# 228 tiny products of nothing at the head of TensorE's program, in place of most of the wide ones

## The chip, the cores and the metric

The kernel runs on one core of a Trainium2 chip. The metric is the device time of one execution in microseconds. TensorE (PE, with its weight loads PEld), VectorE (DVE), ScalarE (ACT), GpSimd (POOL) and SyncE (SP) each run their own program; semaphores and DMA queues tie them together.

## The reference

Three layers follow each other. All is float32.

```python
# attention over 32 memory slots: q, k, v (4, 8, 576, 64), phi (4, 8, 576, 32)
a = np.exp(phi - np.max(phi, axis=2, keepdims=True))
a = a / (np.sum(a, axis=2, keepdims=True) + 1e-09)
k_m = np.einsum('bhsm,bhsd->bhmd', a, k)
v_m = np.einsum('bhsm,bhsd->bhmd', a, v)
scores = np.matmul(q, k_m.transpose(0, 1, 3, 2)) / np.sqrt(64)
attn = softmax(scores)
x = np.matmul(attn, v_m)                    # then (2304, 512)
# gated layer: w_gate, w_val (512, 1536), w_out (1536, 512)
xn = x / np.sqrt(np.mean(x * x, axis=-1, keepdims=True) + 1e-06) * rms_g
x = (silu(xn @ w_gate) * (xn @ w_val)) @ w_out
# second layer: w_in (512, 2048), w_out (2048, 512)
h = x @ w_in
g = np.where(h >= 1, h, np.where(h <= -1, 0.0, (h + 1) ** 2 / 4))
out = g @ w_out
```

## The kernel before, in words

The kernel is one program. Its first part, up to about 440 us, is ordered by a planner that is written out in the kernel (`Agenda`): streams of work (`soft`, `memory`, `pair`, `chunk`, `vw`, `gv`, `out1` and others) yield steps with an engine and a planned duration. The planner takes the step that can start first, by priority among equals, and instructions are issued in that order. The result is a fixed order for every engine; the planned times are not used on the chip.

For each batch b of four, `soft` (line 420) computes the exponentials of phi: DVE takes a maximum (`pm`), PE transposes it (`mps`, line 433), DVE reduces (`gm`) and spreads it (`dg`), PE multiplies by `spread` (line 450), DVE subtracts (line 456), ACT takes the exponential (line 463), and POOL forms the sums `s1`. `memory` (line 492) multiplies the exponentials by k and v: nine steps of eight small float32 products (`kvps`, line 504; 144 PE products in the profile, each with its weight load, because a float32 product is two of them). Its tiles have 64 rows and 32 columns, so four land next to each other in one bank. Two more products (line 517) form the sums of the exponentials. `pair` (line 589) then does the attention of 128 query rows: transposes of q (`qps`, line 612), scores (`sc`, line 630), a softmax on DVE and ACT, transposes (`aTp`, line 672), the product with v's memory (`xp`, line 693), the mean square, and transposes into `Ah` and `Al` (line 717). Inputs arrive by SP's queue in the order phi, k, v of batch 0, q, phi, k, v of batch 1, and so on; there are two buffers each for phi, k with v, and q. Behind the inputs the weights follow in pieces (`raw`), which DVE, ACT and POOL convert in `chunk`.

`heat` (line 477) fills gaps in PE's order with products of a tile of zeros (`zeros`, set by DVE at the start), 128 x 128 weights by 256 columns, which nobody reads. It has the lowest priority. The planner counts PE's planned work in periods of 3.413 us (`TICK`); a wide product of zeros is added in a period only while that period has under 2.09 us of work (`HEAT`), and a period that follows one with over 1.38 us (`WARM`) is planned at full speed, any other at half speed. The stream ends when batch 2's exponentials are planned. Once the attention and the gates are done, PE goes through `out1`, and then a second stage of `hp` and `acc` products that has no planner.

## Time and profile before

| | us |
|---|---|
| median of three runs | 845.07 |
| lowest and highest | 843.63, 845.24 |
| the profiled execution | 843.29 |
| its span, first to last instruction | 841.5 |

Busy time as a share of the span: PE 97%, its weight loads 85%, DVE 53%, ACT 40%, POOL 10%. The span counts from the first to the last instruction; 1.8 us of the profiled execution lie around it. PE and PEld are counted as one instruction each, semaphore instructions are not counted. "issue" in a chain, or as a releaser, is time in which an engine waited for nothing that the profile shows. The DMA table lists traffic by queue; the kind "instruction" is the engines' own program.

### The profile page before, as it was taken

The numbers are of one execution on the slowest core, as the hardware profiler recorded it, in microseconds if no ns is written. First come the engines' busy times: TensorE is split into PE (matmuls) and PEld (weight loads), VectorE is DVE, ScalarE is ACT, GpSimd is POOL, SyncE is SP. The second block draws the span as 40 slices with busy tenths as digits, with TensorE's granted clock in tenths as the row PEclk, the third lists the DMA queues.
The fourth block names the chain that finished last, engine by engine and source line by source line (L and its number), as shares of the span: only waits on it lengthen the run. The fifth ranks groups of instructions, "written<-read, shape, count | busy, mean of one in ns | idle before, by whom it ended". The sixth has DMA issues, their size and how long they took to land.

```text
span 841.5 us, 14910 instructions
## 1 busy us (share of the span) xinstructions
PE 817.0 (97%) x6052; PEld 718.0 (85%) x6052; DVE 449.5 (53%) x788; ACT 337.3 (40%) x635; POOL 82.8 (10%) x133
## 2 busy tenths in 40 slices
PE   7999879999999999999999999999999999999997
PEld 5877767999999999999998888888888888888896
DVE  3678898984776577558214333433343334333443
ACT  1558866763664366435203222222222222222232
POOL 3365400100000000001305100000000000000000
PEclk9999899999999999999999999999999999999999
DMA  9974697885788768786969900100040003000100
GB/s 324 322 245 146 215 309 252 305 280 180 240 281 303 238 225 273 259 268 224 334 221 351 356 0 1 51 1 0 17 134 0 1 1 101 0 1 1 51 1 25
DMA packets 76804, 137.54 MB, mean 163 GB/s; under 512 B 9408, under 2 KB 46272, under 8 KB 76736
## 3 DMA queue, kind: packets, MB, share of 16 engines
q1 hardware_dynamic: 66080, 108.02, 38.7%
q0 software_dynamic: 10496, 28.32, 10.6%
q8 instruction: 47, 0.77, 0.4%
q10 hardware_dynamic: 160, 0.26, 0.1%
q14 instruction: 21, 0.17, 0.1%
HBM read 99.35 MB, written 37.22 MB: 162 GB/s over the span
## 4 chain that ended last, share of the span: by engine, by line
PE 91%; DMA 4%; ACT 2%; DVE 2%; issue 1%; SPq 0%; DVEq 0%; ACTq 0%
PE acc L1129 24%; PE hp L1098 24%; PE ops L920 18%; PE vps L819 8%; PE gps L819 8%; PE vwps L772 3%; PE xp L693 2%; DMA raw<-in_moe_w_val_dram 2%; PE sc L630 2%; DMA kv<-in_v_dram 1%; PE kvps L504 1%; PE qps L612 1%; DMA raw<-in_moe_w_gate_dram 1%; PE heat L484 0%; DVE w L285 0%
## 5 line engine op out<-in xcount | busy, mean ns | idle before, releaser
L1098 PE MATMUL hp<-xh,w 128*128 128x512 f32 (+1 forms) x640 | 193.1, 368 | 0.0
L1129 PE MATMUL acc<-w,gh 128*128 128x512 f32 x576 | 178.4, 391 | 0.0
L1098 PEld LDWEIGHTS hp<-xh,w 128*128 128x128 f32 x640 | 117.0, 188 | 21.5
L1104 DVE SCALAR_TENSOR_TENSOR y<-y 128x512 f32<-128x512 f32 (+1 forms) x80 | 51.1, 639 | 151.4 <-ACT y L1103 151.4
L1129 PEld LDWEIGHTS acc<-w,gh 128*128 128x128 f32 x576 | 107.0, 188 | 22.4
L1098 PE MATMUL hp<-xl,w 128*128 128x512 f32 (+1 forms) x320 | 118.3, 370 | 0.0
L920 PE MATMUL ops<-ah,wo1h 128*128 128x288 f32 x384 | 113.7, 296 | 0.0
L920 PE MATMUL ops<-ah,wo1l 128*128 128x288 f32 x384 | 113.1, 295 | 0.0
L920 PE MATMUL ops<-al,wo1h 128*128 128x288 f32 x384 | 113.1, 294 | 0.0
L1129 PE MATMUL acc<-w,gl 128*128 128x512 f32 x288 | 112.6, 392 | 0.0
L1103 ACT ACTIVATE y<-hp,consts 128x512 f32<-128x512 f32 (+1 forms) x80 | 51.8, 648 | 150.9 <-PE hp L1098 150.9
L1113 ACT ACTIVATE gh<-y 128x512 fp32r<-128x512 f32 (+1 forms) x80 | 47.5, 593 | 137.4 <-PE acc L1129 120.0
L1114 DVE TENSOR_TENSOR gl<-y,gh 128x512 fp32r<-128x512 f32 (+1 forms) x80 | 51.1, 639 | 80.3 <-ACT gh L1113 80.3
L920 PEld LDWEIGHTS ops<-ah,wo1h 128*128 128x128 f32 x384 | 72.0, 188 | 2.5 <-issue 2.5
L920 PEld LDWEIGHTS ops<-al,wo1h 128*128 128x128 f32 x384 | 72.0, 188 | 0.0
L920 PEld LDWEIGHTS ops<-ah,wo1l 128*128 128x128 f32 x384 | 72.0, 188 | 0.0
L1098 PEld LDWEIGHTS hp<-xl,w 128*128 128x128 f32 x320 | 60.3, 188 | 10.8
L1129 PEld LDWEIGHTS acc<-w,gl 128*128 128x128 f32 x288 | 54.0, 188 | 12.3
L819 PE MATMUL vps<-Ah,vwh 128*128 128x288 f32 x192 | 59.4, 309 | 2.4 <-DVE th L875 2.4
L819 PE MATMUL gps<-Ah,vwh 128*128 128x288 f32 x192 | 58.1, 303 | 2.3 <-ACT th L872 2.3
L819 PE MATMUL gps<-Ah,vwl 128*128 128x288 f32 x192 | 57.3, 298 | 0.0
L819 PE MATMUL gps<-Al,vwh 128*128 128x288 f32 x192 | 57.2, 298 | 0.0
(123 smaller groups left out, 1254.1 us busy)
## 6 DMA issues: line engine op xcount, KB each, us to landing
w<-wf_d SPq DMA_DIRECT2D x36, 512.0 KB, 4.9
w<-w_d POOLq DMA_DIRECT2D x36, 512.0 KB, 10.6
w_d<-w2s SPq DMA_DIRECT2D x32, 512.0 KB, 3.8
raw<-in_moe_w_out_dram SPq DMA_DIRECT2D x28, 512.0 KB, 4.8
raw<-in_moe_w_in_dram SPq DMA_DIRECT2D x16, 512.0 KB, 5.1
raw<-in_moe_w_gate_dram SPq DMA_DIRECT2D x12, 512.0 KB, 5.9
raw<-in_moe_w_val_dram SPq DMA_DIRECT2D x12, 512.0 KB, 6.3
wf_d<-w SPq DMA_DIRECT2D x12, 512.0 KB, 3.9
```

Source lines behind the costliest of these rows:

```text
L504: nc.tensor.matmul(out=kvp[g][0][32 * c : 32 * c + 32, 0 : 2 * D], lhsT=ph[gs, c, j, :], rhs=kv[gs, :, c, j, :], start=(j == 0), stop=(j = ...
L630: nc.tensor.matmul(out=scv[rows, z, :], lhsT=qT[:, h, rows], rhs=kmT_t[bb][:, z].rearrange("p j m -> p (j m)"), start=True, stop=True, ski ...
L693: nc.tensor.matmul(out=xp[rows, 256 * g : 256 * g + 256], lhsT=aT[:, i, g, rows], rhs=vbd_t[bb][:, g].rearrange("p h d -> p (h d)"), start ...
L772: nc.tensor.matmul(out=vps[g][0][32 * c : 32 * c + 32, 2 * P * x : 2 * P * x + 2 * P], lhsT=vT[b][hs, c, :], rhs=t[hs, c].rearrange("p i f ...
L819: nc.tensor.matmul(out=p[:, 0:HB], lhsT=wt[:, g, i, :], rhs=at[b][:, g, c], start=(g == 0 and x == 0), stop=(g == 1 and x == 2),)
L920: nc.tensor.matmul(out=p[:, 0:HB], lhsT=wt[:, fc, d], rhs=at[:, c], start=(fc == 0 and x == 0), stop=(fc == NF1 - 1 and x == 2),)
L1098: nc.tensor.matmul(out=hp, lhsT=wt[:, kc, :], rhs=xt[:, kc, 0:n], start=(kc == 0 and x == 0), stop=(kc == KC - 1 and x == 2),)
L1103: nc.scalar.activation(out=y, in_=hp, func=AF.Relu, scale=0.5, bias=half)
L1104: nc.vector.scalar_tensor_tensor(out=y, in0=y, scalar=1.0, in1=y, op0=ALU.min, op1=ALU.mult)
L1113: nc.scalar.activation(out=gh, in_=y, func=AF.Copy)
L1114: nc.vector.tensor_tensor(out=gl, in0=y, in1=gh.bitcast(F32), op=ALU.subtract)
L1129: nc.tensor.matmul(out=acc, lhsT=gt[:, cs], rhs=wt, start=(fc == 0 and x == 0), stop=(fc == NF2 - 1 and x == 2),)
```

## The change

`heat` issues 228 products of 32 x 32 x 64 zeros ahead of its loop, going round the four groups of 32 output partitions of the same bank. Around them it books PE's planned time twice, 3.9 us before they are issued and 2.6 us behind, as a step of kind "Pz" that the planner doesn't lengthen. The loop of wide products follows as it was.

```diff
+BURN = (228, 2.9, 2.6)
...
-                    t *= slow
+                    t *= 1.0 if kind == "Pz" else slow
...
         yield "take", ("bank", HEAT[0])
         t = psum.tile([P, 512], F32, tag=f"b{HEAT[0]}", name="heat")
+        yield "Pz", BURN[1] + 1
+        for n in range(BURN[0]):
+            c = n % 4 * 32
+            nc.tensor.matmul(
+                out=t[c : c + 32, 0:32], lhsT=zeros[0:64, 0:32], rhs=zeros[0:64, 0:32],
+                start=True, stop=True, skip_group_check=True,
+            )
+        yield "Pz", BURN[2]
         while HEAT[1] not in agenda.flags:
             go = yield "heat", 0.1067
```

## Rows read from the trace of the kernel before

**Rows 1.** The page: engines' busy time, the chain's shares, PE's program queue.
```profile
PE 817.0 (97%) x6052; PEld 718.0 (85%) x6052; DVE 449.5 (53%) x788; ACT 337.3 (40%) x635; POOL 82.8 (10%) x133
PE 91%; DMA 4%; ACT 2%; DVE 2%; issue 1%; SPq 0%; DVEq 0%; ACTq 0%
q8 instruction: 47, 0.77, 0.4%
```

**Rows 2.** Stages (length; PE, PEld, DVE, ACT, POOL busy; granted clock; DMA share, GB/s).
```profile
57.00:82.00 25.00, 24.27 (x382) 21.08 (x381) 21.69 (x46) 20.58 (x45) 15.48 (x19) 1.00 0.31 101
140.00:841.00 701.00, 696.26 (x4502) 616.15 (x4494) 347.92 (x591) 252.58 (x464) 33.22 (x54) 1.00 0.44 145
```

**Rows 3.** The chain that ended last in order of time: start, length, what.
```profile
1.77 10.26 DMA kv<-in_v_dram
12.17 2.24 PE kvps L504 x143
15.48 0.33 PE qps L612 x3
15.81 2.86 issue
...
23.66 0.12 PE mps L433
...
27.70 2.25 PE kvps L504 x144
...
41.30 1.47 PE kvps L504 x91
42.77 0.68 issue
...
45.11 1.73 PE xp L693 x8
46.84 0.32 PE kvps L517 x4
...
57.77 2.18 PE kvps L504 x144
```

**Rows 4.** Stages up to the first stop's end, and to the second's.
```profile
0.00:18.60 18.60, 13.01 (x222) 10.03 (x222) 7.43 (x13) 2.44 (x2) 7.03 (x24) 1.00 0.94 316
18.60:43.00 24.40, 23.15 (x381) 20.27 (x382) 14.39 (x32) 11.98 (x23) 9.16 (x12) 0.93 1.09 331
```

**Rows 5.** DMA in windows 16.0:17.2 (two rows), 22.4:23.6, 40.8:42.1, 47.2:48.5, 60.1:61.1 (two rows).
```profile
DMA packets 198, 0.47 MB, mean 390 GB/s; under 512 B 1, under 2 KB 1, under 8 KB 197
q8 instruction: 1, 0.02, 5.7%
...
q8 instruction: 1, 0.02, 5.6%
...
q8 instruction: 1, 0.02, 5.4%
...
q8 instruction: 1, 0.02, 5.5%
...
DMA packets 1, 0.02 MB, mean 16 GB/s; under 512 B 0, under 2 KB 0, under 8 KB 0
q8 instruction: 1, 0.02, 6.5%
```

**Rows 6.** PE in order of time, from the start.
```profile
1.04 6.09 PE L484 MATMUL heat<-zeros 128*128 128x256 bf16 x37 [1.04 <-DVE zeros L355]
```

**Rows 7.** A stage behind the first stop, columns as in rows 2.
```profile
20.00:22.00 2.00, 2.00 (x11) 1.93 (x10) 0.00 (x0) 1.19 (x2) 0.00 (x0) 0.50 1.05 385
```

**Rows 8.** v of batch 1: its issue, its landing after that; DVE's pm of batch 1.
```profile
9.98 2.04 SPq L387 DMA_DIRECT2D kv<-in_v_dram  x1
...
DMA to landing us min/median/max: 13.2/13.2/13.2
...
16.56 2.08 DVE L427 TENSOR_REDUCE pm<-phi 128x128 f32<-128x1152 f32 x1 [0.19 <-DMA phi<-in_phi_dram]
```

## The prediction

> **What bounds the kernel now.** I read the page first. PE is busy for 97% of the span and carries 91% of the chain that ended last; all DMA together has 4% of it [rows 1]. So an edit counts only if it moves PE's own order of work. The table of stages says where that can be: from 140 us to the end PE is busy for 696.26 of 701 us, and nothing there waits. Between 57 and 82 us it is busy for 24.27 of 25 us, and the DMA engines are at a third [rows 2]. In that stretch every engine works through a fixed order and the transfers start when buffers come free, so I see nothing tied to absolute time after about 57 us. A shift of PE's work that stands there should reach the end unchanged. The question is what the change does before 57 us.

> **What is removed and added.** In the planner, 228 tiny products book PE's time up to 6.64 us, over the 2.09 us that HEAT wants in both of the first two planned periods. Of the 37 wide products that open PE's program [rows 6], 36 go, and one is left ahead of the first transpose. From there the plan has the same free times and the same two warm periods, so the order of all later work is the same. PE's program becomes 456 - 72 = 384 instructions longer at its head: 24 KB, which at 390 GB/s is 0.06 us of DMA time. No other queue gets anything.

> **The opening itself.** No row has a 32-column bf16 product of this tile. The nearest are the 144 products of 32 output rows and 128 columns in 2.24 us [rows 3], 15.6 ns each, at full clock. So I bound the 228 between a quarter of 15.6 ns (a quarter of the columns) and twice it (the half clock that rows 7 show elsewhere): 0.9 to 7.1 us, and take 3.6 us, ending near 4.6. About product 222 to 224 ends block 1, and PE waits there. Block 0 ended near product 94, so the packet for block 2 was asked for at about 2 to 2.5 us, when the inputs have just begun; with 3.5 to 6.4 us it is usable at 5.5 to 9. The wide products ended at 7.13 before, and the first transpose came with their end [rows 6]. So this costs 0 to 2 us there, and it is covered: the 144 products that follow wait for v of batch 0 until 12.03 [rows 3], and behind those the chain has 2.86 us that will not be needed. I put this part at 0.

> **Where the block ends fall afterwards.** Counting forward in the old order, less 384:
> - Block 2 ends at about product 92 of the first 144. Its successor was asked for at 5.5 to 9, usable by 9 to 15.4; needed at 12.17 + 92 x 0.0156 = 13.6. Between 0 and 1.8 us late, still covered as above.
> - Block 3 then ends at the second or third of the 144 products that stood at 27.70. The place at 15.81 now has no block end, so the transposes go on and 2.86 us are gained for the moment, with some more since PE's clock need not fall: the granted clock was 0.50 from 20 to 22 us, after that stop [rows 7]. The set can start once v of batch 1 has landed, at 9.98 + 13.2 = 23.2 us [rows 8], and its exponent is done, which before took 27.70 - 23.66 = 4.0 us from the transpose; pm for that is ready at 16.56 + 2.08 = 18.6 [rows 8], near 19.3 behind the products of zeros. So the set starts at about 23.4, 4.3 us early.
> - Block 4 ends at about product 130 of that same set. The sequencer can enter block 4 only when it has passed the wait for v at 23.2, so its successor is asked for at 23.2 and is usable at 23.2 + 6.4 = 29.6. Before, product 130 ran at 27.70 + 130 x 0.0156 = 29.7. The whole gain of 4.3 us is waited away again: -0.1 us.
> - Block 5 ends at about product 27 of the set at 41.30; asked for at 29.6, it is there by 36. The old stop of 0.68 us at 42.77 falls away: -0.7 us, for the moment.
> - Block 6 ends before the last of the eight xp products that end at 46.84 [rows 3]. Its successor is asked for when the sequencer enters block 6, 41.3 to 41.7, and is usable at 47.7 to 48.1. Without the old stop PE would be there near 45.6. So it waits some 2.2 us, and the last xp product ends at 47.7 + 0.25 = 48.0 instead of 46.84: +1.15 us.
> - The next that could be late is asked for near product 45 of the set at 57.77, at 58.5, and by the low end usable at 62.0; it is needed 60 instructions behind that set's end at 59.95, which at that stretch's 763 in 25 us is 61.9 [rows 2, 3]. Nothing is late there, or hardly, and later work needs fewer instructions in a microsecond.

> Sum: 0 - 0.1 - 0.7 + 1.9 = **+1.1 to +1.2 us**, in PE's order at 48 us. What follows (row sums, transposes, the third and fourth memories) starts from that product and from the sums behind it, so I carry it to the end. The profiled execution has a span of 841.5 us and took 843.29, 1.8 us around it; the sum gives a span of 842.65 and 844.4. The median of the three runs is 845.07, 1.8 us above that execution, so in its terms 846.2.

> [...]

> **Rivals.**
> - *The stops go and no new ones come.* If blocks asked for at 23.2 and 41.3 come in 3.5 us, as in idle DMA, the second set ends at 23.2 + 3.5 + 0.2 = 26.9 instead of 29.95, and the later stop is gone too: -3.0 - 0.7 = -3.7 us, 841.4. For it: the first request comes before the inputs fill the queues. Against: over 18.6 to 43.0 the DMA engines are full, share 1.09 [rows 4].
> - *Late blocks cost more.* Each 0.1 us that a block takes beyond 6.4 counts twice, in the second set and again near 46, so the sum passes 1.7 from 6.7 us. With 7.1 us it is +2.5, with 7.7 us +3.7: 847.6 to 848.8. For it: the packet between 40.8 and 42.1 [rows 5] belongs to a block that, counted forward from 18.67, PE entered near 35.8, over 5 us earlier. Against: the packets behind 18.67 and 43.45 came alike, within 0.1 us as far as the windows tell.
> - *Nothing moves by much.* PE passes every block end within 0.5 us because the next block is there, except in places where it would have waited for a buffer or an input anyway (the second set for v at 23.2, the last xp product for its bank near 47): 845.1, from -0.5 to +0.5. For it: 45 of the 47 packets of the kernel before came without a stop that the chain shows; against: 256 instructions pass in 2 us in the sets of 144.

> **How the numbers follow.** A measurement of this kernel can tell about 0.2%, 1.7 us, from no change. Forecast, +0.5 to +1.7: 0.42. Late blocks, over +1.7: 0.25. Little moves: 0.15. Stops gone: 0.18, beyond -1.7. The forecast's upper edge gives 0.02 to slower. So faster 0.18, same 0.40 + 0.15 = 0.55, slower 0.27. The range leaves out the ends of the two outer cases, some 0.1 each: 841.4 to 848.6. The forecast's own is 845.6 to 846.8.

> **What the profile would show.** Right: the stop at 15.81 gone and the granted clock at 1.00 from 18 to 24 us; a stop inside the tiny products near the 223rd; one some 14 products before the second set's end, until 29.6; one before L517 near 46, until 47.7; from 57 us on a constant shift. Wrong: q8's packets within 4 us of a block's start under load, two blocks not being all that is there at first, or a PE order changed beyond the opening.

## The result, and the profile after

The changed kernel takes 850.69 us (median of six, 848.03 to 853.03) against 844.20 for the kernel before (843.63 to 845.24): a ratio of 1.0075, 95% interval 1.0053 to 1.0097. It is 6.5 us slower where +1.1 was forecast and 848.6 was the upper end. The profiled execution took 849.44 us with a span of 847.7, against 843.29 and 841.5. It is one of the quicker of the six: it has a mean granted clock of 0.990, and the four that took 849.88 to 853.03 us have 0.980 to 0.983. What follows is read from the one trace.

The page of the changed kernel, beside [rows 1]: PE's busy time grew by 1.8 us, the chain's share of "issue" from 1 to 2%, and PE's program by two packets.

```profile
PE 818.8 (97%) x6244; PEld 718.7 (85%) x6244; DVE 449.2 (53%) x788; ACT 338.2 (40%) x635; POOL 83.8 (10%) x133
PE 91%; DMA 3%; DVE 2%; ACT 2%; issue 2%; SPq 0%; DVEq 0%; ACTq 0%
q8 instruction: 49, 0.80, 0.4%
```

The chain that ended last in the changed kernel, in order of time (start, length, what); lines of the source are 9 higher than before. It answers to [rows 3].

```profile
1.04 2.02 PE heat L485 x208
3.06 4.90 issue
...
10.63 3.91 PE heat L493 x18
14.54 2.18 PE kvps L513 x144
...
25.63 2.15 PE kvps L513 x130
27.78 2.49 issue
30.27 0.45 PE kvps L513 x14
30.72 2.92 PE sc L639 x16
...
34.15 2.03 PE heat L493 x9
...
44.84 2.18 PE kvps L513 x144
...
49.12 2.26 issue
51.37 0.48 PE xp L702
51.86 0.44 PE kvps L526 x4
52.29 1.90 PE sc L639 x8
...
65.94 2.18 PE kvps L513 x144
...
90.33 1.04 PE vwps L781 x32
...
135.36 5.06 DMA raw<-in_moe_w_gate_dram
...
145.55 0.67 PE vwps L781 x16
```

The stop of 2.86 us among the transposes of q is gone, and so is the one of 0.68 us in the third set of 144 products. In their place PE stops for 4.90 us in the tiny products, 2.49 us behind product 130 of the second set, and 2.26 us ahead of the last xp product. To compare, the same places of the kernel before that were not shown yet:

```profile
29.94 1.93 PE sc L630 x16
...
32.19 1.09 PE heat L484 x9
...
47.15 1.03 PE sc L630 x8
...
82.15 1.04 PE vwps L772 x32
...
128.93 6.91 DMA raw<-in_moe_w_val_dram
...
139.49 0.67 PE vwps L772 x16
```

The 16 sc products took 1.93 us and now take 2.92, nine wide products of zeros 1.09 and now 2.03, the eight sc products 1.03 and now 1.90. None of them waits for anything. The stages of the changed kernel say why (length; PE, PEld, DVE, ACT, POOL busy; granted clock; DMA share, GB/s). The first of them holds the tiny products up to the first stop, 223 products and 224 weight loads:

```profile
0.00:5.00 5.00, 2.02 (x223) 1.92 (x224) 0.40 (x2) 0.18 (x1) 4.11 (x20) 1.00 0.60 188
...
27.70:30.30 2.60, 0.11 (x5) 0.03 (x6) 1.89 (x2) 0.00 (x0) 0.96 (x3) 1.00 1.05 386
30.30:34.00 3.70, 3.70 (x34) 3.38 (x34) 0.00 (x0) 0.00 (x0) 0.00 (x0) 0.65 1.16 289
34.00:37.50 3.50, 3.50 (x19) 2.98 (x19) 2.84 (x12) 0.36 (x1) 1.71 (x2) 0.50 1.11 199
...
45.00:49.10 4.10, 4.10 (x155) 3.39 (x139) 3.08 (x6) 1.91 (x5) 3.87 (x6) 1.00 1.09 372
49.10:51.40 2.30, 0.04 (x2) 0.03 (x1) 0.00 (x0) 0.15 (x2) 0.84 (x1) 1.00 1.07 340
51.40:55.00 3.60, 3.60 (x19) 3.36 (x19) 2.62 (x6) 0.69 (x2) 2.11 (x4) 0.57 1.09 347
55.00:59.00 4.00, 4.00 (x22) 4.00 (x21) 1.27 (x4) 1.79 (x3) 1.02 (x2) 0.53 0.26 85
```

PE was almost idle in each of the two later stops, and behind each the granted clock fell to 0.50 while PE was busy all the time, from 31.4 to 38.3 and from 51.9 to 58.7 us; the rows at 0.65, 0.57 and 0.53 hold part of it. Between the two it was back at 1.00, from 45.0 to 49.1 us. From the starts in the two chains the shift of PE's order can be split (after minus before; the first column names where a stage ends):

| PE's order up to | before | after | shift | added in the stage |
|---|---|---|---|---|
| start of the first set of 144 | 12.17 | 14.54 | +2.37 | +2.37: opening |
| start of the second set | 27.70 | 25.63 | -2.07 | -4.44: old stop gone, and the half clock behind it |
| end of the second set | 29.94 | 30.72 | +0.78 | +2.85: new stop |
| start of the third set | 41.30 | 44.84 | +3.54 | +2.76: half clock |
| sums of the third set | 46.84 | 51.86 | +5.02 | +1.48: stop of 2.26 for one of 0.68 |
| start of the fourth set | 57.77 | 65.94 | +8.17 | +3.15: half clock |
| first vwps | 82.15 | 90.33 | +8.18 | 0 |
| vwps, 16 products | 139.49 | 145.55 | +6.06 | -2.12: waits for weights |
| end of the span | 841.5 | 847.7 | +6.2 | +0.1 |

So the stops themselves, with the ones they replace, leave 0.78 + 1.48 = 2.3 us, the half clock behind them costs 2.76 + 3.15 = 5.9 us, and 2.1 us are given back where PE waits for the weights to come by DMA (`raw`) anyway. The product at 122.31 us comes at 130.47 us in the changed kernel, still 8.16 us late; the 2.1 us come back between that and 137 us.

### The profile page after: what moved, and what is told of

Its sections match the earlier page's. It is cut to its first block, busy times and chain, and to the rows that moved or that the text cites. A ratio compares the mean times of both kernels' runs of the same rounds, so it can differ in the third digit from the quotient of the medians.

```text
span 847.7 us, 15294 instructions
## 1 busy us (share of the span) xinstructions
PE 818.8 (97%) x6244; PEld 718.7 (85%) x6244; DVE 449.2 (53%) x788; ACT 338.2 (40%) x635; POOL 83.8 (10%) x133
## 4 chain that ended last, share of the span: by engine, by line
PE 91%; DMA 3%; DVE 2%; ACT 2%; issue 2%; SPq 0%; DVEq 0%; ACTq 0%
PE acc L1138 23%; PE hp L1107 23%; PE ops L929 18%; PE vps L828 8%; PE gps L828 7%; PE vwps L781 2%; DMA raw<-in_moe_w_val_dram 2%; PE sc L639 2%; PE xp L702 2%; PE heat L493 1%; PE kvps L513 1%; PE qps L621 1%; DVE w L286 1%; DMA raw<-in_moe_w_gate_dram 1%; DVE w L281 1%
## 5 line engine op out<-in xcount | busy, mean ns | idle before, releaser
L1138 PEld LDWEIGHTS acc<-w,gh 128*128 128x128 f32 x576 | 107.0, 188 | 22.4
```

The costliest lines, as they stand in the source:

```text
L1138: nc.tensor.matmul(out=acc, lhsT=gt[:, cs], rhs=wt, start=(fc == 0 and x == 0), stop=(fc == NF2 - 1 and x == 2),)
```

## The experiments

Theory A: program blocks come late, and the stops of PE and the half clock behind them make the loss. Theory B: the new opening makes it (the tiny products, or the late and slow start), and it is passed on. Theory C: the waits alone cost.

**292 tiny products.** Half a block more moves the later block ends back to where they were before, with the opening unchanged.

```diff
-BURN = (228, 2.9, 2.6)
+BURN = (292, 2.9, 2.6)
```

> 292 tiny products in place of 228: 128 instructions more, half a block, so the later block ends stand where they stood in the kernel before; the opening stays that of the changed kernel. Theory A (late blocks, and the half clock that follows each stop of PE, make the loss): no stop in the second set of 144 products nor ahead of the last xp near 47 to 50; the old stop among the transposes of q is back, some 2.4 us later than before because the first set starts at about 14.5; 845.5 to 848. Theory B (what opens the program costs: the first transpose late, 18 wide products at half clock, the first set 2.4 us late, and all of it is passed on): 850 to 852 as the changed kernel. Theory C (only the waits cost, and the opening is covered): 844 to 845.

Measured 848.42 us (847.24 to 849.71), ratio 1.0065 (1.0041 to 1.0089). Its chain in order of time:

```profile
17.95 2.54 issue
...
29.79 2.25 PE kvps L513 x144
...
43.39 2.18 PE kvps L513 x144
...
58.82 3.79 PE kvps L513 x144
```

The places came as counted: the old stop is back among the transposes of q, and the second and third sets run through (43.39 is 2.1 us behind before, not 3.5). The time is 0.4 us over A's range. In the profiled execution PE's order was 2.5 us behind at 140 us, which is in A's range, but in part by another way than A's: 1.05 us stood at the fourth set (58.82 for 57.77), and that set then took 3.79 us for 2.18, at a granted clock of 0.50 from 59 to 62 us, with no stop for the program ahead of it. PE's order lost 2.6 us more in waits between 325 and 346 us that no other profile has at that size. Why is open for both.

**192 tiny products, then the 36 wide ones.** As many instructions as the changed kernel, with PE kept busy at the opening.

```diff
-BURN = (228, 2.9, 2.6)
+BURN = (192, 2.9, 2.6)
...
+        for n in range(36):
+            nc.tensor.matmul(
+                out=t[:, 0:256], lhsT=zeros[:, 0:P], rhs=zeros, start=True, stop=True,
+                skip_group_check=True,
+            )
```

> 192 tiny products and then the 36 wide ones of the kernel before, as many instructions as in the changed kernel: later block ends as in the changed kernel, but PE is kept busy at the opening. Theory A: the clock rises by about 8 us and the first set starts at 12.2 to 13, and yet the second set stops near its 130th product until about 30 and PE stops again ahead of the last xp, both followed by half clock; 848.5 to 852. Theory B: with the opening repaired 844 to 846. Theory C: both stops, without the price of the clock: 845 to 846.

Measured 852.54 us (848.62 to 854.47), ratio 1.0108 (1.0075 to 1.0140), 0.5 us over A's range and far from B's. Its chain, from the slowest of the four executions:

```profile
24.57 2.15 PE kvps L518 x130
26.72 3.46 issue
30.18 0.68 PE kvps L518 x14
30.86 3.60 PE sc L644 x16
...
50.01 1.83 issue
```

This ends theory B in the form that a slow opening costs. The second set starts 1.06 us earlier than in the changed kernel, stops at the same product, and goes on at 30.18 against 30.27: the time at which the block can be used decides, not PE's start. The sc products behind the stop take nearly twice their time again (3.60 us for 1.93).

**No tiny products, and no wide ones at the head.**

```diff
-BURN = (228, 2.9, 2.6)
+BURN = (0, 2.9, 2.6)
```

> No tiny products, and the 36 wide ones stay out: the program is 72 instructions shorter than before. Counted forward, blocks end at product 64 of the first set, in the products by spread of batch 1, near product 102 of the second set, just ahead of the third set and near its 127th product, and after the fourth set. Theory A: the first transpose near 7.0, the first set at 12.5 to 13.5, no stop among the transposes of q, a stop under 1 us in the second set, one of 2 to 4 us near the end of the third set with half clock after it; 846 to 849. Theory B in the form that the tiny products cost: 844 to 845. In the form that the missing warm-up costs: 850 to 852.

Measured 843.98 us (840.08 to 849.32, ten executions), ratio 1.0016 (0.9989 to 1.0043): below A's range, and by its time alone for B. Its chain has one stop over 0.4 us, where the count put it, behind product 127 of the third set:

```profile
37.78 1.94 PE kvps L513 x127
39.72 2.46 issue
42.18 0.48 PE kvps L513 x17
...
44.98 0.32 PE kvps L526 x4
```

In this execution, 840.08 us, no half clock followed that stop (1.00 from 42.20 to 45.00 us). Over the ten executions the time goes with the mean granted clock: 848.18, 849.17 and 849.32 us had 0.983, 0.982 and 0.986, the other seven 0.989 to 0.994 and 840.08 to 845.86 us. A mean of 0.983 for 0.993 is some 17 us more at half clock, which on PE-bound work would cost 8 us (an estimate); there is no trace of the slow ones. I had let every stop be followed by half clock; it need not be.

**256 tiny products.** To part A from B: the tiny products are there, even 28 more, and the blocks end where those of the last run do.

```diff
-BURN = (228, 2.9, 2.6)
+BURN = (256, 2.9, 2.6)
```

> The changed kernel with 256 tiny products in place of 228: 28 more of the same, 56 instructions, so that all later blocks end where those of the run without tiny products do (which is 512 instructions shorter). Theory A: the stop in the second set falls from 2.49 to under 1 us, the stop ahead of the last xp goes, one of 2 to 3 us comes near product 127 of the third set; 844 to 847, so some 5 us faster than the changed kernel by 28 more products of nothing. Theory B (the tiny products themselves cost): 850 to 852.

Measured 844.36 us (841.58 to 851.55, ten executions), ratio 1.0009 (0.9988 to 1.0031). That is in A's range: 28 more products of nothing take 6 us off the changed kernel, and theory B has nothing left. Its chain, with the stop again behind product 127:

```profile
39.67 1.94 PE kvps L513 x127
41.61 2.44 issue
44.05 0.48 PE kvps L513 x17
...
48.52 0.32 PE kvps L526 x4
```

This and the run before are a pair that prices the clock in one place: the same products, a stop of 2.44 and of 2.46 us at the same product, and from the end of the stop to the sums 44.98 - 42.18 = 2.80 us in the one, 48.52 - 44.05 = 4.47 us in the other. The stage between, first without and then with the tiny products:

```profile
42.20:45.00 2.80, 2.80 (x31) 2.12 (x30) 0.69 (x1) 1.29 (x3) 0.68 (x1) 1.00 1.04 390
```

```profile
44.05:48.50 4.45, 4.45 (x31) 3.35 (x30) 0.69 (x1) 1.28 (x3) 0.72 (x1) 0.62 1.08 373
```

31 products each, at 1.00 and at 0.62 of the clock: 1.67 us from the end of the stop to the sums. Theory C, by which the stops cost their length alone, is out.

**Nine wide products made tiny.** The nine that ran 2.03 us at half clock, in the changed kernel.

```diff
+                made += 1
+                if 54 < made <= 63:
+                    c = made % 4 * 32
+                    nc.tensor.matmul(
+                        out=t[c : c + 32, 0:32], lhsT=zeros[0:64, 0:32], rhs=zeros[0:64, 0:32],
+                        start=True, stop=True, skip_group_check=True,
+                    )
+                    continue
                 nc.tensor.matmul(
                     out=t[:, 0:256], lhsT=zeros[:, 0:P], rhs=zeros, start=True, stop=True,
```

> The changed kernel with the nine wide products of zeros behind the sums of batch 1 (2.03 us in the changed kernel at half clock, 1.09 us in the kernel before) made tiny: as many instructions, so block ends as in the changed kernel. Theory A: the stop in the second set stays, the transposes of q behind the nine products start some 1.5 to 1.9 us earlier, the later stop ahead of the last xp moves with them, and the end comes 1 to 2 us earlier than in the changed kernel: 848.5 to 850. Theory C (the clock costs nothing of its own, the nine products fill a wait): same as the changed kernel.

Measured 849.64 us (847.24 to 851.09), ratio 1.0076 (1.0052 to 1.0100): in A's range, but not to be told from the changed kernel by time. Its chain:

```profile
27.11 3.41 issue
30.52 0.45 PE kvps L522 x14
...
34.08 2.90 PE qps L630 x12
...
48.08 2.30 issue
```

The transposes start 2.1 us earlier than the 36.19 us of the changed kernel, and the late stop moves by 1.0 us (49.12 to 48.08) with the third set (44.84 to 43.80). Nine wide products of filler cost nearly twice their price where the granted clock had fallen to 0.50 (2.03 us for 1.09).

**Block ends moved ahead of the third set**, with and without tiny products at the head.

```diff
-BURN = (228, 2.9, 2.6)
+BURN = (0, 2.9, 2.6)          # 256 in the other run
...
+                made += 1
+                if 54 < made <= 63:
+                    for n in range(7 if made <= 57 else 6):
+                        c = n % 4 * 32
+                        nc.tensor.matmul(
+                            out=t[c : c + 32, 0:32], lhsT=zeros[0:64, 0:32], rhs=zeros[0:64, 0:32],
+                            start=True, stop=True, skip_group_check=True,
+                        )
+                    continue
```

> As the run without tiny products (36 wide ones left out), and in place of the nine wide products behind the sums of batch 1 there are 57 tiny ones: 96 instructions more at that place, so that the block end just ahead of the third set of 144 products moves into the transposes of q before it, and the next one from product 127 of that set to about product 79. Theory A (late blocks and the half clock behind the stops): the stop of 2.46 us in the third set goes or falls under 0.5 us, no stop over 1 us is left before 57 us, the second set starts near 23.7 and the third near 37, and the executions lie closer together: 838.5 to 841.5. If the stops of PE cost nothing by themselves: 843 to 845, as the run without tiny products.

> 256 tiny products at the head, and the 57 tiny ones in place of the nine wide ones: block ends as in the run that has the 57 alone, but with the opening of the changed kernel (first transpose after 8 us, first set at 13.3 to 14.5). Theory A: no stop over 1 us behind the opening, 840 to 843. Theory B: 849 to 852.

Measured 843.02 us (840.32 to 843.80, twelve executions), ratio 0.9985 (0.9973 to 0.9998), and with 256 tiny products 844.55 us (841.13 to 847.70), ratio 1.0008 (0.9990 to 1.0026). Both miss A's range. The chain of the first:

```profile
32.00 1.41 issue
...
41.41 2.18 PE kvps L523 x144
```

The stop left the third set, but the 96 instructions that moved it also use up a block sooner, and PE stops among the transposes instead. The third set starts at 41.41 and not near 37. With 256 tiny products the same stop of 1.41 us stands at 32.34. The first median lies where stops that cost nothing by themselves were to put it (843 to 845), but it does not speak for that: a stop was left, with the granted clock at 0.50 from 33.8 to 37.2 us behind it. The executions do lie closer together with the move than without it: 3.5 us from lowest to highest against 9.2, and with 256 tiny products 6.6 against 10.0. The kernel before spreads over 5.7 us in 29 executions, so only the first is closer than that. The first of the two has the lowest median here, by 0.15% below the kernel before, which is less than the 0.2% that I would call a gain.

## Why the prediction was wrong

- *The mechanism, blocks of 256 instructions:* right. Every stop lay where it was counted: the tiny products stop after the 224th weight load, the second set behind product 130, the last xp alone behind the stop. Counted with PE's semaphore instructions, the stops of the changed kernel come after 449, 1217 and 1729 instructions of the trace, those of the kernel before after 449 and 1217. Up to 70 us the chains of the nine kernels have 22 pieces of "issue" of 0.3 us or more, and each stands at 449 or a multiple of 256 later. The first, at 449, lies between one block and two, so the two blocks at the start are an estimate of mine: 512 would need 63 instructions ahead that the trace does not record, and no run shows those.
- *The time that a block takes:* right. Under load 6.4 us was worked out. In the changed kernel v of batch 1 had landed at 23.7 (issued at 10.20, 13.5 us before), and PE went on at 30.27: 6.6 us. The third set, in which the block before the stop begins at product 24 (45.06), started at 44.84, and PE went on at 51.37: 6.3 to 6.5 us. The rival of slow blocks (from 6.7 us) did not come true; its sign came from something else.
- *The opening at 0:* right in effect, wrong in size. The tiny products took 2.02 / 223 = 9 ns each (bounds 4 to 31, taken 15.6), the block was usable at 7.96 (bounds 5.5 to 9), and the first set started 2.37 us late, over the 1.8 allowed, since the 18 wide products ahead of it took 3.91 us. That is 217 ns each, near the 226 ns of the nine at half clock, though the profile's granted clock from 8.4 to 14.5 us reads 1.00. The second set's stop covered it all, as the run with the wide products kept shows.
- *The second set, -0.1:* measured +0.78. The set started at 25.63 and not at 23.4, since the late opening was passed on so far; that cost nothing, as PE had to wait for the block anyway. The block was usable 0.7 us later (30.27 for 29.6), and the 14 products left took 0.45 us for the 0.2 counted.
- *The last xp, +1.15 in all:* the stages with stops add 0.78 + 1.48 = 2.3 us. Mis-sized by a factor of two, 1.1 us.
- *The step that failed:* each new stop was priced at its own length, and the work behind it at full clock, so the price of the clock was put at nothing. The prediction read half clock behind the old stop [rows 7], and booked that it would go; it did not ask what the two new stops would do to the clock. The half clock behind them cost 2.76 + 3.15 = 5.9 us, over twice the stops. The old stop's half clock, from 18.6 to 22 us, slowed PE's own transposes as well (the second eight took 1.70 us there and 1.15 in the changed kernel); its end is part of the 4.44 us by which the second set came earlier, and its own stop took 2.85 of these back. Nothing takes back what the half clock behind the two new stops cost before 122 us. With 5.9 us for the clock and 1.1 more for the stops the sum is +8.2, the shift measured at the fourth set (+8.17).
- *The shift carried unchanged from 57 us on:* held to 82 us (+8.17, +8.18), and again from 140 us to the end (+6.06, +6.2). Between, where PE waits for the weights' DMA, 2.1 us came back. The prediction read only [rows 2] and skipped 82 to 140 us, where PE is busy for 47.73 of 58 us.
- *The rival by which nothing moves:* the stops of 2.49, 2.26 and 4.90 us speak against it. Other block ends come without a stop, also within the sets: the first and the third set of the changed kernel each hold one and take 2.18 us.
- *"Stops gone":* not reached by any run; moving block ends removed one stop and made another. A likely reason, argued and not tested: under load blocks come at 256 instructions in 6.4 us, 40 in a microsecond, and PE's order asks for nearly as many on the mean (763 from 18.6 to 43.0 us is 31, before) and for more in the sets of 144.

## What to carry to other kernels

In these runs TensorE, where it waited "for nothing" at instruction counts a multiple of 256 apart, was waiting for its program: the three stops of the changed kernel ended at 7.96, 30.27 and 51.37 us, each 1.3 to 1.6 us behind the end of a packet of the queue of kind "instruction" (6.57, 28.94 and 49.81). In another kernel, count instructions, look for the queue of kind "instruction", and find out which dense sets of small products the block ends fall on. Then price a stop of PE with what follows it: the granted clock behind the stop, on work that is PE-bound, can cost more than the stop (5.9 us for 2.3 here). Adding instructions at the head of the program was not local in these runs; 28 products of nothing, some 0.25 us of work, made 6 us of difference.

## What the runs showed of the hardware that was not expected

- The same stop of about 2.45 us was followed by half clock in one profiled execution and not in another (44.05 to 48.50 at 0.62, 42.20 to 45.00 at 1.00). Ten executions each of these two kernels spread over 10.0 and 9.2 us, those of the kernel before over 5.7 us in 29. Of the 12 stops of 1.4 us or more behind the openings, in nine traces, 10 have a fall of the granted clock to 0.50 within 2.5 us of their ends.
- The clock also falls without such a stop: in the fourth set with 292 tiny products (3.79 us for 2.18), and in each of the nine traces once between 84 and 98 us (to 0.50 from 86.8 in the kernel before, from 96.3 in the changed one). So the stops are not its only cause, and what decides whether a stop is followed by half clock is open.
- Products of 64 x 32 by 32 columns, going round four groups of output partitions, start 9 ns apart (2.02 us for 223), below the 15.6 ns of the float32 ones with 128 columns (2.24 us for 143).
- The runs fit a sequencer that asks for a block when it enters the one before, and that a wait for a semaphore in its way delays: in the three runs with the stop in the second set, v of batch 1 landed at 23.7, 23.8 and 24.0 us, and PE went on 6.6, 6.4 and 6.5 us later, though the set had started at 25.63, 24.57 and 24.96.
